# Gate weights in two K halves, an earlier gate transfer, and one parameter transpose at the start of an SSM + SwiGLU kernel

## Chip, cores, metric

The kernel runs on one core of one Trainium2 chip. The metric is device time in microseconds (us). Each kernel is run several times. One execution of each is also profiled; the profile's "span" is some 1.8 us shorter than the time. All runs used here are fast, and that only means that a run isn't over 1.5% above the fastest of its kernel.

## The reference, cut to what matters

```python
xn = layernorm(x)                                   # x: 2048 x 512, bf16
A  = 2 * Re(C @ scan(Lam_bar, B_bar @ xn)) + xn * Dskip   # state space part, P = 512
B  = (silu(xn @ w_gate) * (xn @ w_up)) @ w_down           # F = 1376
out = x + A + B
```

The sequence is worked in four chunks of 512 rows. Only the start of chunk 0 is changed: four tiles of x (128 x 512 each) are loaded, normalized and transposed on chip, and the first six tiles of `w_gate` (6 x 128 of the 1376 columns) are multiplied with them, tile by tile of x ("quarters"). K is the dimension that is summed over, here the 512 columns of x in four K tiles of 128. "Gate" and "up" loads and matmuls are those of `w_gate` and `w_up`; the matmuls write to PSUM. Later chunks of x are transposed by DMA.

## The kernel before

The loads, in issue order on two queues (SyncE is the default, `eng="act"` is ScalarE's queue):

```python
FQ = 4 * 128                                       # FH0 = 6 * 128
act_q = [pload("ld_ldt", 2, A_log_dt)]             # 1 KB, ScalarE's queue
dma("ld_x0", ...); dma("ld_x1", ...)               # 128 KB each, SyncE
act_load("ld_wgA0", wg[:, 0:2, 0:FQ], ...)         # 256 KB, K tiles 0-1, ScalarE
dma("ld_x2", ...)
act_load("ld_wgA1", wg[:, 2:4, 0:FQ], ...)         # 256 KB, K tiles 2-3, ScalarE
dma("ld_wg0", wg[:, :, FQ:FH0], ...)               # 256 KB, SyncE
dma("ld_x3", ...)
pload("ld_lim", ...); pload("ld_lre", ...)         # 1 KB each, ScalarE
dma("ld_wu0", ...); dma("ld_wg1", ...); dma("ld_wu1", ...); dma("ld_x4", ...)
# ... later: transposing loads of B (2), of xn chunk 1, of C (2), then x tiles 8-11
```

TensorE's start: warm-up matmuls on a constant, the transposes of tile 0 in two halves, three more warm-ups, then the quarters:

```python
pe_warm(10)
xt_tile_fine(0, parts=2, wbank=...)      # half, 1 warm-up, half; each half copied by ScalarE
pe_warm(3, 256, ...)
for q in range(4):
    for ii, (i, bk) in enumerate(tiles):                    # six tiles
        if q == 0 and ii == 2:
            params_t(...)                                   # three 4x128 transposes
            ln_chunk0_rest(...)
        if q < 3 and ii == (4 if q == 0 else 2):
            xt_tile_fine(q + 1)                             # next tile: 4 transposes, one copy
        # ... 4 matmuls over K for tile i, quarter q
```

A small scheduler orders the instructions of VectorE, ScalarE and GpSimd by estimates; TensorE and SyncE keep the order of the program.

## Time and profile before

| | before |
|---|---|
| time, median of 3 runs | 180.34 us (180.32 to 180.59) |
| span of the profiled run | 178.4 us |
| TensorE busy / on the chain that ended last | 98% / 95% |
| first gate weight load / first up matmul on the chain | 6.03 / 13.15 us |

The prediction shows the chain of waits and the weight-load row. One more view is needed below, the timeline of VectorE (start, length, engine, line, operation, output and inputs, count, and in brackets the idle time ahead and what ended it):

```profile
2.95 0.69 DVE L466 BATCH_NORM_STATS2 st<-x_sb 128x6 f32<-128x512 bf16 x1 [2.95 <-DMA x_sb<-in_A_x_dram]
...
3.96 0.68 DVE L466 BATCH_NORM_STATS2 st<-x_sb 128x6 f32<-128x512 bf16 x1
4.74 0.60 DVE L485 TENSOR_SCALAR xn_sb<-x_sb,mv,rstd 128x256 bf16<-128x256 bf16 x2
```

The first line is tile 0's arrival, 2.95. The second is tile 1. The third is both halves of tile 0's normalization.

### The profile page before, as it was taken

The numbers are of one execution on the slowest core, as the hardware profiler recorded it, in microseconds if no ns is written. First come the engines' busy times: TensorE is split into PE (matmuls) and PEld (weight loads), VectorE is DVE, ScalarE is ACT, GpSimd is POOL, SyncE is SP. The second block draws the span as 40 slices with busy tenths as digits, with TensorE's granted clock in tenths as the row PEclk, the third lists the DMA queues.
The fourth block names the chain that finished last, engine by engine and source line by source line (L and its number), as shares of the span: only waits on it lengthen the run. The fifth ranks groups of instructions, "written<-read, shape, count | busy, mean of one in ns | idle before, by whom it ended". The sixth has DMA issues, their size and how long they took to land.

```text
span 178.4 us, 2380 instructions
## 1 busy us (share of the span) xinstructions
PE 174.3 (98%) x919; PEld 83.6 (47%) x927; DVE 160.8 (90%) x273; ACT 86.5 (48%) x107; POOL 12.7 (7%) x24
## 2 busy tenths in 40 slices
PE   8899999999999999999999999999999999999994
PEld 2694444444444444444444444444444444444743
DVE  3987759998799999999999999999999999999733
ACT  3379899899796991061565651000965620000000
POOL 3351300002200000300000000000000000000000
PEclk9999999999999999999999999999999999999999
DMA  4994646669360000002420000001100000001112
GB/s 152 343 365 103 142 82 73 152 174 353 108 118 4 0 0 0 0 0 91 101 48 0 0 0 4 0 0 65 53 0 4 0 0 0 0 0 62 44 44 88
DMA packets 23410, 12.37 MB, mean 69 GB/s; under 512 B 15112, under 2 KB 23400, under 8 KB 23400
## 3 DMA queue, kind: packets, MB, share of 16 engines
q1 hardware_dynamic: 22832, 11.70, 24.5%
q10 hardware_dynamic: 568, 0.53, 1.0%
q8 instruction: 7, 0.11, 0.3%
q14 instruction: 3, 0.02, 0.0%
HBM read 6.46 MB, written 2.10 MB: 48 GB/s over the span
## 4 chain that ended last, share of the span: by engine, by line
PE 95%; DMA 1%; DVE 1%; issue 1%; ACT 0%; POOL 0%
PE pb L713 36%; PE pb L901 21%; PE pb L818 15%; PE pb L914 15%; PE pb L752 3%; PE pb L781 2%; DMA x_sb<-in_A_x_dram 1%; PE pb L791 1%; PE pb L543 1%; DVE st L466 0%; ACT xnT L549 0%; POOL rstd L478 0%; PE pb L450 0%; DVE xn_sb L485 0%; DVE x_sb L919 0%
## 5 line engine op out<-in xcount | busy, mean ns | idle before, releaser
L858 DVE TENSOR_TENSOR_SCAN rot<-sm,car,rot 128x512 bf16<-128x512 f32 x32 | 39.0, 1266 | 0.1
L901 PE MATMUL pb<-wd,hT 128*128 128x512 bf16 (+3 forms) x194 | 38.1, 355 | 0.2
L713 PE MATMUL pb<-xnT,wu 128*128 128x512 bf16 x160 | 37.3, 379 | 0.0
L713 PE MATMUL pb<-xnT,wg 128*128 128x512 bf16 x136 | 32.0, 379 | 0.0
L914 PE MATMUL pb<-W,hss 128*128 128x512 bf16 (+2 forms) x140 | 28.1, 355 | 0.2
L818 PE MATMUL pb<-xnT,BT 128*128 128x512 bf16 x128 | 28.1, 379 | 0.0
L901 PEld LDWEIGHTS pb<-wd,hT 128*128 128x128 bf16 (+1 forms) x198 | 18.5, 98 | 19.9
L725 ACT ACTIVATE sg<-pb 128x1024 bf16<-128x1024 f32 x20 | 20.2, 1022 | 10.9 <-PE pb L713 10.6
L713 PEld LDWEIGHTS pb<-xnT,wu 128*128 128x128 bf16 x160 | 15.6, 98 | 18.6
L771 ACT ACTIVATE uf<-pb 128x1024 bf16<-128x1024 f32 x20 | 20.4, 1022 | 7.1 <-PE pb L713 6.6
L713 PEld LDWEIGHTS pb<-xnT,wg 128*128 128x128 bf16 x136 | 13.2, 98 | 16.4 <-issue 0.8
L914 PEld LDWEIGHTS pb<-W,hss 128*128 128x128 bf16 x144 | 13.5, 98 | 14.3
L818 PEld LDWEIGHTS pb<-xnT,BT 128*128 128x128 bf16 x128 | 12.5, 98 | 15.1
L825 ACT ACTIVATE u_sb<-pb 128x1024 bf16<-128x1024 f32 x16 | 16.3, 1026 | 3.9 <-PE pb L818 3.5
L919 DVE TENSOR_TENSOR x_sb<-pb,x_sb 128x512 bf16<-128x512 f32 (+2 forms) x18 | 10.9, 621 | 4.9 <-PE pb L914 4.9
L773 DVE TENSOR_TENSOR hT<-sg,uf 128x1024 bf16<-128x1024 bf16 x20 | 13.4, 676 | 1.9 <-ACT uf L771 1.9
L466 DVE BATCH_NORM_STATS2 st<-x_sb 128x6 f32<-128x512 bf16 x16 | 10.2, 683 | 4.9 <-DMA x_sb<-in_A_x_dram 4.9
L495 ACT ACTIVATE xn_sb<-x_sb,nmr,rstd 128x512 bf16<-128x512 bf16 x8 | 5.9, 802 | 10.0 <-DVE nmr L492 10.0
L800 ACT ACTIVATE sg<-pb 96x1024 bf16<-96x1024 f32 x2 | 2.0, 1020 | 17.4 <-PE pb L781 17.4
L849 DVE TENSOR_TENSOR rot<-u_sb,sin 128x2048 bf16<-128x2048 bf16 x8 | 9.7, 1214 | 0.0
L849 DVE TENSOR_TENSOR rot<-rot,sin 128x2048 bf16<-128x2048 bf16 x8 | 9.7, 1214 | 0.0
L849 DVE TENSOR_TENSOR rot<-u_sb,cosT 128x2048 bf16<-128x2048 bf16 x8 | 9.7, 1212 | 0.0
(71 smaller groups left out, 138.6 us busy)
## 6 DMA issues: line engine op xcount, KB each, us to landing
out_dram<-x_sb SPq DMA_DIRECT2D x15, 128.0 KB, 1.7
x_sb<-in_A_x_dram SPq DMA_DIRECT2D x3, 512.0 KB, 7.4
wd<-in_B_w_down_dram SPq DMA_DIRECT2D x1, 1280.0 KB, 7.0
wu<-in_B_w_up_dram SPq DMA_DIRECT2D x1, 768.0 KB, 6.4
wg<-in_B_w_gate_dram SPq DMA_DIRECT2D x1, 608.0 KB, 7.7
wu<-in_B_w_up_dram SPq DMA_DIRECT2D x1, 608.0 KB, 8.8
x_sb<-in_A_x_dram SPq DMA_DIRECT2D x4, 128.0 KB, 3.0
wg<-in_B_w_gate_dram ACTq DMA_DIRECT2D x2, 256.0 KB, 3.8
```

What stands on the lines that cost most here:

```text
L466: return g.add("dve", lambda e, a=a: e.bn_stats(out=st[:, a, :], in_=x_sb[:, a, :]), reads=[("x", a)], writes=[("st", a)], name="bnst%d" % ...
L713: inst = e.matmul(pbank[0:fs, bk, :].rearrange("p (j t) -> p j t", j=4), lhsT=w[:, kt, i * 128:i * 128 + fs], rhs=xnT[:, c % 2, :, kt, :], ...
L725: g.add("act", lambda e: e.activation(out=sg[rows, sl, 0:n, :].rearrange("p a t -> p (a t)"), in_=pair_f32(rows, bk, 512 * n), func=AF.Sil ...
L771: g.add("act", lambda e: e.activation(out=uf[rows, ul, 0:n, :].rearrange("p a t -> p (a t)"), in_=pair_f32(rows, bk, 512 * n), func=AF.Ide ...
L773: g.add("dve", lambda e: e.tensor_tensor(out=hT[rows, hb, i0:i0 + n, :], in0=sg[rows, sl, 0:n, :], in1=uf[rows, ul, 0:n, :], op=ALU.mult), ...
L818: inst = e.matmul(pbank[:, bk, :].rearrange("p (j t) -> p j t", j=4), lhsT=BT[:, ri, kt, pt * 128:(pt + 1) * 128], rhs=xnT[:, c % 2, :, kt ...
L825: g.add("act", lambda e: e.activation(out=u_sb[:, us].rearrange("p r t -> p (r t)"), in_=pair_f32(slice(0, 128), b0), func=AF.Identity), r ...
L849: tt = lambda out, a, b, op, r, w, nm: g.add("dve", lambda e: e.tensor_tensor(out=out, in0=a, in1=b, op=op), reads=r, writes=w, name="%s_% ...
L858: g.add("dve", lambda e, A0=A0, A1=A1, k=k, ri=ri, pt=pt: e.tensor_tensor_scan(out=A1[:, k, ri, :], data0=rr[:, pt:pt + 1].to_broadcast([1 ...
L901: inst = e.matmul(pbank[:, bk, 0:nc_], lhsT=hT[0:fs, hb, i, lt * 128:(lt + 1) * 128], rhs=wd[0:fs, i, c0:c0 + nc_], start=(i == 0), stop=F ...
L914: inst = e.matmul(pbank[:, bk, 0:nc_], lhsT=hss[:, hb, pt, ri, lt * 128:(lt + 1) * 128], rhs=W12[:, ri, pt, c0:c0 + nc_], start=False, sto ...
L919: g.add("dve", lambda e, bk=bk, a=a, c0=c0, nc_=nc_: e.tensor_tensor(out=x_sb[:, a, c0:c0 + nc_], in0=pbank[:, bk, 0:nc_], in1=x_sb[:, a, ...
```

## The change

The intent: start the gate matmuls with the first half of K as soon as half of tile 0 and half of the weights are there, close the hole at the edge of each quarter, and take the parameter transposes out of the gate stream.

```diff
-        FQ = 4 * 128
-        act_q = [pload("ld_ldt", 2, A_log_dt)]
         dma("ld_x0", ...); dma("ld_x1", ...)
-        act_load("ld_wgA0", wg[:, 0:2, 0:FQ], ...)
+        act_q = [dma("ld_wgA0", wg[:, 0:2, 0:FH0], ..., 256 * FH0 * 2, eng="act")]
+        act_q.append(dma("ld_wgA1", wg[:, 2:4, 0:FH0], ..., eng="act", order=(act_q[-1],)))
+        pload("ld_ldt", 2, A_log_dt)              # SyncE
+        pload("ld_lim", 1, A_Lambda_im)
+        pload("ld_lre", 0, A_Lambda_re)
         dma("ld_x2", ...)
-        act_load("ld_wgA1", ...); dma("ld_wg0", ...)
         dma("ld_x3", ...)
-        act_q.append(pload("ld_lim", ...)); act_q.append(pload("ld_lre", ...))
 ...
-        pe_warm(10)
+            pe_warm(9, bk=wbank)
+            ln_first()                            # stats 0, stats 1, first half of tile 0
+            xt_tile_fine(0, bridge=bridge)        # half; params_t and rest of layernorm; half
+            pe_warm(1, 256, wbank)
             for q in range(4):
+                steps = [(i, bk, 2 * kh, 2 * kh + 2) for kh in range(2) for i, bk in tiles]
+                #  (last quarter: halves for two tiles, whole K for four)
+                for n, (i, bk, k0, k1) in enumerate(steps):
+                    if q < 3 and n == 8:
+                        xt_tile_fine(q + 1)       # two copies of half a tile
```

The three parameter rows now lie in one 12 x 128 tile and are transposed by one instruction. (Some order hints for ScalarE and VectorE are cut here.)

## The prediction

> **What bounds the kernel now.** I read the page first, for the engine that carries the end. The busy shares and the chain that ended last:
>
> ```profile
> PE 174.3 (98%) x919; PEld 83.6 (47%) x927; DVE 160.8 (90%) x273; ACT 86.5 (48%) x107; POOL 12.7 (7%) x24
> ...
> PE 95%; DMA 1%; DVE 1%; issue 1%; ACT 0%; POOL 0%
> ```
>
> TensorE is the bound: 95% of the chain. DMA, VectorE and the rest together hold 5% of 178.4 us, about 9 us, at the two ends. The change touches only the first 13 us, so next I read the chain in order of time there (start, length, what):
>
> ```profile
> 0.79 2.13 DMA x_sb<-in_A_x_dram
> ...
> 6.06 0.69 PE pb L752 x8
> 6.76 0.08 issue
> 6.83 0.21 PE pb L457 x3
> 7.04 0.55 PE pb L752 x8
> 7.60 0.24 PE pb L543 x4
> 7.86 0.61 ACT xnT L549
> 8.46 0.05 issue
> 8.51 0.62 PE pb L752 x8
> ...
> 10.92 2.23 PE pb L752 x40
> 13.15 12.09 PE pb L713 x56
> ```
>
> Until 6.06 the chain is x tile 0, its layernorm, its transpose and its copy out of PSUM. From 6.06 to 13.15 are the 96 small gate matmuls, and they are interrupted twice. From 13.15 TensorE has no hole: 56 up matmuls take 12.09 us, 216 ns each. The weight-load row of the timeline shows the interruptions best[...]:
>
> ```profile
> 6.03 0.55 PEld L752 LDWEIGHTS pb<-xnT,wg 128*128 128x128 bf16 x8 [0.27 <-DMA wg<-in_B_w_gate_dram]
> 6.80 0.15 PEld L457 LDWEIGHTS pb<-ident,prow 4*128 4x128 bf16 x3 [0.22 <-issue]
> 6.97 0.45 PEld L752 LDWEIGHTS pb<-xnT,wg 128*128 128x128 bf16 x8
> ...
> 8.51 0.45 PEld L752 LDWEIGHTS pb<-xnT,wg 128*128 128x128 bf16 x8 [0.41 <-ACT xnT L549]
> ```
>
> The first gate load waited 0.27 us for weights, three parameter transposes stand in the stream, and the second quarter waited 0.41 us for the ScalarE copy of tile 1. The duration of that copy, by form (256 wide is the shortest, 512 the median):
>
> ```profile
> L549 ACT ACTIVATE xnT<-pb x5: 377/597/597, 5.5 to 11.0; 128x512 bf16<-128x512 bf16 x3, 128x256 bf16<-128x256 bf16 x2
> ```
>
> **What the Trainium skill says.** "DMA: Bandwidth & Descriptors", section "Issuing engines are not separate DMA queues": transfers started by SyncE and ScalarE run on the same 16 DMA engines and interleave; another issuer saves only issue time. The trace agrees: in the half-microsecond table DMA is 95% busy or more from 3.5 to 6.5 us while both issuers are active. The same page, "Queues, rings and completion order", has each engine alternate between queues packet by packet; no view of this trace shows packets of one transfer. "TensorE: Matmul & The Clock Gate", Part 1, gives 107 ns per 128-column matmul cold and 56 ns warm, with some 3.4 us of activity to warm. Here ten 512-wide warm-up matmuls come 0.43 us apart, the cold rate, and the 40 gate matmuls in 2.23 us are 56 ns each, the warm one; the clock turned at about 5.2 us. The clock row says full speed throughout, so it doesn't show this and only durations do.
>
> **The change, part by part.**
>
> First, the parameter transposes. Removed from the gate stream: three, with the hole ahead of them. On the weight-load row that is the hole 0.22 plus 0.15 plus 0.02 until the next gate load, 0.39 us on TensorE's path. Added: one 12x128 transpose between the two halves of tile 0, where TensorE waits for VectorE anyway. It needs three tiny transfers that SyncE now issues as numbers 3 to 5. Issues there are about 0.45 us apart from 0.79, so the last leaves at about 2.6; with the 2.1 us that x tile 0 took it lands at about 4.7, before the first transpose at 5.23. Cost expected on the path: 0.
>
> Second, halves of K. The six tiles of a quarter first take K 0-1, then K 2-3: 12 matmuls of 56 ns, 0.67 us, need only the first half of the copy and of the weights. A whole-tile copy of 0.60 us becomes two of 0.38, so the first matmul can start 0.22 us sooner after it. The next tile's transposes also move ahead of 8 matmuls at the end of each quarter, 8 x 56 = 0.45 us, against a first copy of 0.38 plus a few hundredths of hand-over. So the 0.41 us hole should close. The second copy (another 0.38) lies beside the 0.67 us of first halves. The split first tile also lost about 0.08 us (8 matmuls in 0.69 us where later groups take 0.62); that goes. Matmuls and transposes stay as many: 96 x 56 ns + 12 x 55 ns = 6.04 us, against 7.09 now.
>
> Third, the order of VectorE. The second half of tile 0 moves behind the statistics of tile 1: 0.17 + 0.15 us with 0.04 between, so about 0.35 later. Its transpose goes to about 5.75 and its copy ends near 6.35; the matmuls that need it come at 6.03 + 0.67 = 6.70. Hidden. Tile 1 then needs parameter copy 0.17, statistics of tile 2 0.68 and normalization 0.41 after about 5.65: ready near 6.95. Its transposes are wanted 16 x 56 = 0.89 us after the first gate matmul, 6.92-6.95. This is almost equal, so I charge 0.1 us for a remaining hole. Later tiles cost VectorE 0.68+0.41+0.17+0.15, 1.41 us, below TensorE's 24 x 56 + 4 x 55, 1.56 us: no further hole.
>
> Fourth, transfers. The first gate half grows from 256 to 384 KB and leaves ScalarE at 0.79 instead of 1.38, because the little parameter load (0.56 us) no longer stands before it. The weights' 0.27 us wait should end. But x tile 0 leaves at the same 0.79, and a fine view of DMA rates shows that it moved at 300 to 420 GB/s around 2.2-2.5 us, nearly alone. With a gate transfer beside it, it gets about half: 128 KB at some 400 GB/s is 0.3 us, so it comes up to 0.3 us later, 0.25 charged. It heads the chain, so all behind it moves. The first gate matmul is then bound by the copy of tile 0: that ended at 5.54 + 0.38 = 5.92 and now near 6.17; with hand-over the first load is at about 6.2 instead of 6.03, a loss of 0.17 us.
>
> **The sum.** Gains 0.39 + 0.41 + 0.08 = 0.88; losses 0.17 + 0.10 = 0.27; net about 0.6 us. The gate stage should run from about 6.2 to 12.5 instead of 6.06 to 13.15. Behind it TensorE has no hole to fill or make: the up weights (issued at 3.20, landing 6.4 us later, 9.6) are early; the transposed B matrices land at 19.02 + 4.9 = 23.9, and their second half is needed at 25.24 + 0.86 = 26.1; the last scan output ends at 164.9 against its use at 169.1. Each slack is larger than 0.6, so the gain should reach the end: 180.34 - 0.6 = 179.7 us.
>
> **Rivals.** (a) *The wait turns into a DMA wait.* Before its second gate half the chip must move 768 KB of gate weights and 256 to 512 KB of x, some 1.0 to 1.3 MB; summing the half-microsecond rates of before, 1.05 MB had moved by 5.5 us and 1.34 MB by 6.5. The need is at about 6.85. Usually enough, by little; x tile 2, issued near 2.9 instead of 1.7, is also close to its use at 5.9. If this goes wrong, 0.3 to 0.6 us return: 180.0 to 180.3. (b) *Start later than charged*, because x tile 0 loses more, or the parameter transfer is late and blocks TensorE's in-order stream before the second half: 180.2 or a little over. (c) *Clock*: nine warm-ups end at about 4.7, leaving 0.5 us idle instead of 0.24. If the turn is put off, matmuls cost 107 instead of 56 ns for some time: +0.05 us each, 1.7 us over a 3.4 us window, thus about 181.4. Against it: 3.8 us of warm-up is still over the skill's 3.4. (d) *The gain is hidden later*: VectorE is almost 100% busy from 50 to 150 us. Against it are the slacks above. It would give 180.3. (e) *No charge is real*, full gain: 179.4.
>
> **Range and chances.** (a), (b), (d) fill 180.0 to 180.4, (e) and a weight wait that I undervalued 179.2 to 179.5. Three runs of before differ by 0.27 us. Range 179.1 to 180.5. A 2% change is 3.6 us; the whole of 6.06-13.15 holds only 1.05 us of holes, and the whole clock risk is 1.7. Faster by over 2%: 0.01; within 2%: 0.98; slower: 0.01.
>
> **What the profile after would show.** The first gate weight load at 6.1 to 6.3, released by the copy and not by DMA; no load of parameters inside the gate stream; no ScalarE release of over 0.1 us in it; the first up matmul at 12.4 to 12.7; statistics of tile 0 starting at 3.1 to 3.25 instead of 2.95; an unbroken TensorE chain from then on. Wrong would be: a gate load released by the weights' or x's DMA for over 0.2 us, gate matmuls 107 ns apart, or a hole after 13 us that was not there.

## The result, and the profile after

The changed kernel took 181.57 us (median of 6, 180.83 to 181.88), the kernel before in the same rounds 180.5 (6 runs, 180.32 to 180.97). Ratio 1.0051, 95% interval 1.0026 to 1.0076. A ratio is the mean time of one kernel's fast runs over that of the other's in the same rounds, so it is not quite the ratio of the medians. By the 2% rule that is "same", but it is slower, about 1.9 us over the forecast of 179.7 and outside its range. The profiled run of the changed kernel was the slowest of its six (181.88), so the 1.7 us explained below are that run's; the medians differ by 1.07.

The chain of waits of the changed kernel, in order of time (start, length, what):

```profile
1.25 3.59 DMA x_sb<-in_A_x_dram
...
5.96 0.37 PE pb L538 x2
6.33 0.12 PE pb L449
6.45 0.35 PE pb L538 x2
6.79 0.21 PE pb L444
7.01 1.71 PE pb L756 x16
8.71 0.43 PE pb L538 x4
9.14 1.92 PE pb L756 x24
...
14.87 12.09 PE pb L709 x56
```

The first up matmul stands at 14.87 instead of 13.15: 1.72 us later, and the span is 1.7 us longer (180.1 for 178.4). So the whole loss is made in the first 15 us. The first line is the transfer of x tile 1. L538 are transposes of x, L449 the parameter transpose, L756 the gate matmuls. The first 16 gate matmuls take 1.71 us, 107 ns each; the 40 gate matmuls at the end of the gate stage before took 56 ns each. Four transposes take 0.43 instead of 0.22.

TensorE's matmul and weight-load rows in its timeline, two answers:

```profile
5.96 0.37 PE L538 MATMUL pb<-ident,xn_sb 128*128 128x128 bf16 x2 [1.13 <-DVE mv L461]
```

```profile
6.80 1.65 PEld L756 LDWEIGHTS pb<-xnT,wg 128*128 128x128 bf16 x16 [0.17 <-ACT xnT L544]
...
14.65 1.23 PEld L709 LDWEIGHTS pb<-xnT,wu 128*128 128x128 bf16 x7
```

The first up load of the kernel before, for comparison:

```profile
12.93 0.37 PEld L713 LDWEIGHTS pb<-xnT,wu 128*128 128x128 bf16 x3
```

TensorE stood still for 1.13 us ahead of its first transpose. The first gate load is at 6.80 (before: 6.03), and the first up load at 14.65 (before: 12.93), so the gate stage takes 7.85 us instead of 6.90. The 1.72 us are thus 0.77 of later start and 0.95 of a longer stage. VectorE's timeline says why the start is late:

```profile
3.43 0.69 DVE L457 BATCH_NORM_STATS2 st<-x_sb 128x6 f32<-128x512 bf16 x1 [3.43 <-DMA x_sb<-in_A_x_dram]
...
4.87 0.69 DVE L457 BATCH_NORM_STATS2 st<-x_sb 128x6 f32<-128x512 bf16 x1 [0.34 <-DMA x_sb<-in_A_x_dram]
5.48 0.33 DVE L488 TENSOR_SCALAR xn_sb<-x_sb,mv,rstd 128x256 bf16<-128x256 bf16 x1
```

Tile 0 arrives 0.48 us later than before. Tile 1 also arrives late (4.85), and as its statistics stand ahead of tile 0's normalization in VectorE's order, that normalization begins at 5.48 instead of 4.74.

What the clock does isn't visible in the clock row of this profile, which reads full speed throughout; only the 107 ns tell.

### The profile page after: what moved, and what is told of

Its sections match the earlier page's. It is cut to its first block, busy times and chain, and to the rows that moved or that the text cites. A ratio compares the mean times of both kernels' runs of the same rounds, so it can differ in the third digit from the quotient of the medians.

```text
span 180.1 us, 2383 instructions
## 1 busy us (share of the span) xinstructions
PE 175.8 (98%) x921; PEld 84.8 (47%) x921; DVE 160.5 (89%) x273; ACT 87.1 (48%) x110; POOL 12.7 (7%) x24
## 4 chain that ended last, share of the span: by engine, by line
PE 95%; DMA 2%; DVE 1%; SPq 0%; issue 0%
PE pb L709 36%; PE pb L906 21%; PE pb L919 15%; PE pb L823 15%; PE pb L756 4%; DMA x_sb<-in_A_x_dram 2%; PE pb L786 2%; PE pb L796 1%; PE pb L538 1%; DVE st L457 0%; SPq L384 0%; DVE x_sb L924 0%; DVE xn_sb L488 0%; PE pb L444 0%; PE pb L449 0%
## 5 line engine op out<-in xcount | busy, mean ns | idle before, releaser
L863 DVE TENSOR_TENSOR_SCAN rot<-sm,car,rot 128x512 bf16<-128x512 f32 x32 | 38.9, 1265 | 0.0
L906 PE MATMUL pb<-wd,hT 128*128 128x512 bf16 (+3 forms) x198 | 38.8, 355 | 0.0
```

The lines of the kernel that those rows point to most:

```text
L863: g.add("dve", lambda e, A0=A0, A1=A1, k=k, ri=ri, pt=pt: e.tensor_tensor_scan(out=A1[:, k, ri, :], data0=rr[:, pt:pt + 1].to_broadcast([1 ...
L906: inst = e.matmul(pbank[:, bk, 0:nc_], lhsT=hT[0:fs, hb, i, lt * 128:(lt + 1) * 128], rhs=wd[0:fs, i, c0:c0 + nc_], start=(i == 0), stop=F ...
```

## Experiments

Theory 1 (clock): the hole ahead of the first transpose keeps TensorE's clock slow into the gate stage. Theory 2 (data): late x tiles and weights alone explain the loss. Times are medians (lowest to highest), ratios to the kernel before of the same chip and rounds.

| run | time, us | ratio (95%) |
|---|---|---|
| e1: 13 warm-ups | 180.88 (180.52 to 181.38) | 1.0024 (1.0005 to 1.0043) |
| e2: gate transfer later again | 181.04 (180.61 to 183.07) | 1.0022 (1.0004 to 1.0041) |
| e3: before with 7 warm-ups | 181.41 (180.35 to 182.6) | 1.0046 (1.0013 to 1.008) |
| e4: tile 0 ahead of tile 1 | 181.95 (180.57 to 182.54) | 1.0068 (1.0037 to 1.01) |
| e5: repaired version | 180.46 (180.13 to 180.91) | 1.0002 (0.9981 to 1.0023) |
| e6: e5, gate transfer at once | 180.48 (180.38 to 180.91) | 1.0005 (0.9987 to 1.0024) |
| e7: e5, whole K | 181.68 (181.26 to 182.36) | 1.0071 (1.0049 to 1.0093) |
| e8: changed kernel again | 181.79 (180.74 to 182.2) | 1.0062 (1.0036 to 1.0088) |
| e9: e5, x tiles 8-11 earlier | 180.42 (180.21 to 181.5) | 1.0006 (0.9986 to 1.0026) |
| e10: before, x tiles 8-11 earlier | 180.72 (180.4 to 180.92) | 1.0014 (1.0 to 1.0028) |
| e11: e9, gate weights shared out | 180.01 (179.87 to 180.31) | 0.9974 (0.996 to 0.9988) |
| e12: e11, x tiles 8-11 late again | 180.71 (180.45 to 182.29) | 1.0034 (1.0 to 1.0067) |
| e13: e11 again | 180.21 (179.75 to 180.62) | 0.9978 (0.9957 to 0.9999) |

All results were correct. e1 to e4 shared a chip and rounds (before: 180.45, 180.03 to 181.06), as did e5 to e8 (before: 180.46), e9 and e10 (180.41), and e12 and e13 (180.52); e11 ran by itself (180.51).

### e1: fill the hole

```diff
-            pe_warm(9, bk=wbank)
+            pe_warm(13, bk=wbank)
```

> The changed kernel with 13 instead of 9 warm-up matmuls, so that TensorE has no hole of 1.13 us ahead of its first transpose (4.83 to 5.96 us in the changed kernel's trace). Theory 1 (clock): the hole put off the turn from 107 to 56 ns per gate matmul until about 10.2 us. Then here nearly all gate matmuls come 56 ns apart, the gate stage takes 6.2 to 6.4 us from its first load, the first up matmul stands at 13.0 to 13.4 and the time is 179.9 to 180.5, spread some 0.6. Theory 2 (data): the slow gate matmuls and the later end come from late x tiles and late weights, filling the hole changes nothing: first up matmul at about 14.9, time 181.2 to 181.8.

The x tiles were nearly as late as in the changed kernel (statistics at 3.25 and 4.82, there 3.43 and 4.87), and TensorE's weight-load row reads:

```profile
6.65 0.90 PEld L756 LDWEIGHTS pb<-xnT,wg 128*128 128x128 bf16 x16
...
12.97 2.96 PEld L709 LDWEIGHTS pb<-xnT,wu 128*128 128x128 bf16 x15
```

The stage takes 12.97 - 6.65 = 6.32 us with the same data order and nearly the same late x, against 7.85. The 16 loads take 0.90 instead of 1.65. So 1.53 us of the changed kernel's stage are the slow clock, and without it the stage is 0.58 shorter than before (6.90). A count without e1 agrees: by the chain of the changed kernel some 27 gate matmuls took 107 instead of 56 ns, and four transposes 0.43 instead of 0.22 us, together 1.6 us. Theory 2 fell in the profile. But the two profiles are the fastest of e1's six runs and the slowest of the changed kernel's. The times fell by less: the ratio from 1.0051 to 1.0024, some 0.5 us (0.7 by the medians, which are of different rounds), and the two intervals overlap. The 180.88 is above the expected 180.5; part of that is explained by e5.

### e3: make the hole in the kernel before

```diff
-    warm=10,
+    warm=7,
```

> The kernel before with 7 instead of 10 warm-up matmuls and nothing else: a hole of about 1.4 us ahead of the first transpose at 5.23, as the changed kernel has, with the old data order and the old transfers. Clock theory: gate matmuls 107 ns apart until some time between 8.5 and 12, +1 to +2 us: 181.3 to 182.4. Data theory: same time as before, 180.2 to 180.8.

The time went from 180.45 to 181.41. The stretches of the profiled run (length, TensorE busy and instructions, granted clock, DMA share, GB/s) show the clock here, because it changes twice within the run. The first fence is its first transpose:

```profile
5.17 0.27 PE L543 MATMUL pb<-ident,xn_sb 128*128 128x128 bf16 x2 [1.39 <-DVE xn_sb L485]
```

```profile
6.00:6.50 0.50, 0.50 (x8) 1.00 1.30 308
6.50:7.00 0.50, 0.20 (x4) 0.87 0.78 264
7.00:7.50 0.50, 0.44 (x7) 0.50 1.03 349
...
10.00:11.00 1.00, 1.00 (x18) 0.86 1.08 359
```

The gate matmuls began at the full clock, dropped to half at about 6.9 and came back at about 10.3, some 3.4 us later. TensorE had stood still for 1.39 us before its first transpose (and the drop falls into a second hole, of 0.36 us from 6.70 on). Only three warm-ups had been left out, so in this run a hole of this size was enough. Not every run pays: the six runs were 180.35, 180.53 and 181.4 to 182.6.

### e8: the changed kernel again

> The changed kernel once more, on the chip and in the rounds of its repaired versions. Clock theory: its time depends on where the turn of the clock falls, which differs from run to run, so a spread of 1 us or more (180.5 to 182.5), median 181.3 to 181.8, and a first up matmul in the profile anywhere from 13.2 to 15. Data theory: spread as small as that of the kernel before (0.3 to 0.6 us) and the gate matmuls slow in every profile.

Six runs between 180.74 and 182.2; with the first six, twelve between 180.74 and 182.2, a spread of 1.46 us. The spread is what the clock theory had said. The profile again has the first 16 gate matmuls in 1.71 us and the first up matmul at 14.79; slow gate matmuls in both profiles are what both theories allow. By the distances of the matmul starts, the turn to 56 ns falls at 10.2 and 10.0 in the two profiles of this kernel, at 4.9 in e1, at 3.8 in e5: it isn't tied to the kernel's start. "TensorE: Matmul & The Clock Gate", Part 1, of the Trainium skill offers a reason: the activity window is 3.4 us long and free-running. The runs agree with it: in all profiles but those of the changed kernel and e2 the first turn fell between about 3.5 (e12) and 6.7 us (e10), less than one window apart. That the window is the cause no run here shows.

### e2: give x its head start back

```diff
-        act_q = [dma("ld_wgA0", ...)]
+        act_q = [pload("ld_ldt", 2, A_log_dt, eng="act")]
+        act_q.append(dma("ld_wgA0", ..., order=(act_q[-1],)))
-        pload("ld_ldt", 2, A_log_dt)
```

> The changed kernel with one small parameter load put back on ScalarE's queue ahead of the gate weights, so that the gate weights leave about 0.55 us after x tile 0 as before (and SyncE issues one transfer less ahead of x tile 2). If the gate transfer beside it made x tile 0 late, its statistics start at 2.95 to 3.1 again instead of 3.43 and those of tile 1 don't wait for its transfer; first transpose at 5.2 to 5.4, hole ahead of it 0.4 to 0.6 us. By the clock theory the clock then turns in time or nearly so: first up matmul 12.4 to 13, time 179.6 to 180.2. By the data theory alone the first up matmul moves by the 0.7 us of the x tiles only: 14.2, time 180.9. If x tile 0 stays at 3.4, the delay has another cause than the neighbour. The order of later VectorE work changes a little with this edit; TensorE's chain after 13 us should stay without holes.

The statistics of tile 0 began at 2.85 and those of tile 1 at 3.86 without a wait: the gate transfer beside them is what made x late. But the first up matmul came at 16.06 in the profiled run, which was the slowest of the seven (the other six took 180.61 to 181.1). Its chain has a new wait, and its weight loads show the slow clock, until about 12.6:

```profile
5.12 0.37 PE pb L538 x2
5.50 1.06 issue
6.55 0.16 PE pb L449
```

```profile
9.08 2.61 PEld L756 LDWEIGHTS pb<-xnT,wg 128*128 128x128 bf16 x24
```

The gate stage took 9.0 us (from 6.84 to 15.84), so the clock did not turn in time as expected: the hole had only moved behind the first transposes. L449 is the parameter transpose. It stands ahead of the second half's transposes in TensorE's program, and TensorE stood still 1.06 us in front of it although the second half of tile 0 was normalized by 5.52. The profile names no releaser here; in e4's it names the parameter transfers (0.57 us for one of them). The last of these 1 KB loads was issued at 2.13 us in e2 and 2.41 in e4, and TensorE began with them only at 6.52 and 6.26.

### e4: tile 0's normalization ahead of tile 1's statistics

```diff
-            last = bn_st(1, order=(last,))
-            hold["last"] = ln_half(0, 0, order=(last,))
+            last = ln_half(0, 0, order=(last,))
+            hold["last"] = bn_st(1, order=(last,))
```

> The changed kernel with the first half of tile 0's normalization ahead of the statistics of tile 1 on VectorE, so that the late transfer of x tile 1 (landing 4.85) no longer holds the first transpose. First transpose at about 5.5 instead of 5.96, hole 0.7 instead of 1.13 us. Data theory: 0.45 us sooner, if tile 1 doesn't become the limit: 181.1; as tile 1's chain is unchanged, the gain can shrink to 0. Clock theory: the same, unless a hole of 0.7 us no longer puts off the clock's turn; then 179.7 to 180.3.

The first transpose moved to 5.60 as expected, but the first gate load stayed at 6.89: the second half of tile 0 waits behind tile 1's statistics, and the parameters held TensorE until 6.26. The profiled run had the fast clock throughout, other runs took up to 182.54, the three slowest with a mean granted clock of 0.991. So this is no repair; the hole was only cut into pieces.

### e5 and e6: repaired, and what the head start costs

The repaired version has e2's edit, the other two small loads behind x tile 3, the parameter transpose after the second quarter, and two short warm-ups in its old place:

```diff
             def bridge():
-                params_t(pbk)
-                ln_chunk0(pbk)
+                pe_warm(2, 256, wbank)
+                ln_chunk0()                     # without the parameter copy
-            pe_warm(9, bk=wbank)
+            pe_warm(10, bk=wbank)
 ...
+                if q == 1:
+                    params_t(xt_pair[0]); ln_rest(xt_pair[0])
```

> The changed kernel with three repairs: one small parameter load ahead of the gate weights on ScalarE's queue (x tiles 0 and 1 get their head start), the other two small loads behind x tile 3 and the parameter transpose after the second quarter (in the run with the head start alone it blocked TensorE until 6.5 us), ten warm-ups and two short ones between the halves of tile 0. Theory: late x tiles plus holes that put off the clock's turn ate the gain; with both gone the first gate load comes at about 6.0, the gate stage takes 6.2 us, first up matmul at 12.2 to 12.6, time 179.4 to 180.0, ratio to the kernel before 0.994 to 0.997. Rival (weights): with the gate weights 0.5 us later the second half of K now waits for its weights; first up matmul 12.8 or later, ratio 0.998 to 1.000.

> As the repaired version, but the gate weights again leave at once (the small load goes to SyncE behind x tile 3), with 13 warm-ups to fill the longer wait for tile 0. This isolates what the head start of the gate weights costs when no hole is left to blame: if the gate transfer beside x is the cause, statistics of tile 0 at 3.25 to 3.45 and of tile 1 waiting until about 4.8, first gate load 6.6 to 6.8, about 0.7 us later than in the repaired version, time 180.1 to 180.7. If x tiles come late for another reason, the two versions are equal.

In e5 the front worked as expected: first gate load at 5.90, first up load at 12.54 (before 12.93). In e6, with the gate transfer at once, the statistics are back at 3.61 and 5.00, the first gate load at 6.76 and the first up load at 13.21. So the head start is worth 0.67 to 0.86 us to the front, and it was the neighbour that delayed x. But both took the same time, 180.46 and 180.48. e5 lost its lead later, in two rows of its timeline (the first fence ScalarE, the second weight loads):

```profile
46.80 2.93 ACT L481 ACTIVATE xn_sb<-x_sb,nmr,rstd 128x512 bf16<-128x512 bf16 x4 [1.96 <-DVE nmr L478]
49.63 1.00 ACT L781 ACTIVATE uf<-pb 128x1024 bf16<-128x1024 f32 x1
```

```profile
50.68 1.41 PEld L711 LDWEIGHTS pb<-xnT,wu 128*128 128x128 bf16 x8 [1.07 <-ACT uf L781]
```

Four normalizations of x tiles 8 to 11 stand in one block on ScalarE, and the copy that frees PSUM comes after them. TensorE's weight loads wait 1.07 us, where the kernel before has no hole. The cost is less: from the first up matmul (12.75 on the chain) to the end e5 takes 178.8 - 12.75 = 166.05 us, the kernel before 178.4 - 13.15 = 165.25, so 0.8 us were lost. Those x tiles land at 41.2 us, because their load comes after five transposing loads that run one after the other from 14.85 us on; this chain doesn't get shorter when TensorE starts sooner (before, they landed at 40.6). The weight loads of e1 and e4 have the same hole (0.63 and 0.81 us); e6, whose tiles happened to land by 38.9, has none.

### e7: the repaired version with whole K

```diff
-                    steps = [(i, bk, 2 * kh, 2 * kh + 2) for kh in range(2) for i, bk in tiles]
+                steps = [(i, bk, 0, 4) for i, bk in tiles]
-                    if q < 3 and n == 8:
+                    if q < 3 and n == 4:
```

> The repaired version with the gate matmuls of a tile over the whole K again, six groups of four in each quarter (the copies out of PSUM stay in halves). If the halves of K close the hole at the quarter's edge, this version has holes of 0.2 to 0.4 us at the second quarter and starts its first gate matmuls about 0.3 us later: first up matmul 0.5 to 0.9 us later, time +0.4 to +0.9 over the repaired version. If the halves of K give nothing, the two are equal within 0.2 us.

The weight-load row has the holes that the halves close:

```profile
6.81 0.91 PEld L755 LDWEIGHTS pb<-xnT,wg 128*128 128x128 bf16 x16 [1.04 <-ACT xnT L546]
...
8.75 0.90 PEld L755 LDWEIGHTS pb<-xnT,wg 128*128 128x128 bf16 x16 [0.36 <-ACT xnT L546]
```

The first up load comes at 13.93 against 12.54, and the time is 181.68 against 180.46. The halves of K are worth 1.2 us in this arrangement (1.39 at the first up load, of which e5 loses more later), more than the 0.4 to 0.9 expected, probably because the start needs all 768 KB of weights. (The 1.04 us are put down to the copy, which had ended at 6.31. The weights' second half is the likelier releaser: in e5, with the same loads, the matmuls that need it began at 6.74. The profile doesn't name it.)

### e9 and e10: move the later load

```diff
         def loads_stage_b2():
+            dma("ld_x8", x_sb[:, 8:12, :], ...)
             dma("ld_cre", ..., xpose=True)
             dma("ld_cim", ..., xpose=True)
-            dma("ld_x8", x_sb[:, 8:12, :], ...)
```

> The repaired version with the load of x tiles 8 to 11 moved ahead of the two transposing loads of C, instead of behind them. Theory (second wall): in the repaired version those tiles land at 41.2 us, so that their four normalizations sit on ScalarE at 46.8 to 49.7 and hold the copies out of PSUM; TensorE then waited 1.07 us at 50.7 and lost what it had gained in the first 13 us. Here the tiles land at about 31.5 to 32, the normalizations run earlier, the wait at 50.7 is gone and the span is the first up matmul (12.5 to 12.8) plus 165.2: 177.7 to 178.2, time 179.4 to 180.0, ratio to the kernel before 0.994 to 0.998. Rival: the wait only moves (ScalarE is short of time for tables and copies anyway, or the B and C matrices come late), and the time stays at 180.3 to 180.6.

> Control: the kernel before with the same move of the load of x tiles 8 to 11 and nothing else. It has no hole on TensorE at 50 us, so the move alone should give nothing: time within 0.2 us of the kernel before, ratio 0.999 to 1.001, first up matmul at 13 as before. If it gains as much as the repaired version does, the load order is a change of its own and says nothing on where the gain of the first 13 us went.

e9 has no hole at 50 us any more; its normalizations now lie between 37 and 42.7. But it took 180.42, as its front had a hole of its own:

```profile
7.45 0.24 PEld L758 LDWEIGHTS pb<-xnT,wg 128*128 128x128 bf16 x4 [0.65 <-issue]
```

Its chain puts this down to the gate weights, which landed at 7.34. In e5 the same hole was 0.16. The control e10 gained nothing (ratio 1.0014, a little over the expected 1.001), so the moved load alone is no gain. Its profile also shows that the start of the kernel before varies: its clock turned only at about 6.7, and its first up matmul stood at 13.70, not at 13.15. The time of e9 by itself couldn't show that the hole at 50 mattered, as its front was late too.

### e11, e12, e13: both at once, and the later wall alone

e11 shares the second half of the gate weights out:

```diff
-        act_q.append(dma("ld_wgA1", wg[:, 2:4, 0:FH0], ..., eng="act"))
+        act_q.append(dma("ld_wgA1", wg[:, 2:3, 0:FH0], ..., eng="act"))
 ...
+        dma("ld_wgA2", wg[:, 3:4, 0:FH0], ...)     # SyncE, behind x3, ahead of the up weights
```

> The version of the run before last (repairs, x tiles 8 to 11 loaded earlier), with the second half of the gate weights shared out: K tile 2 stays on ScalarE's queue, K tile 3 goes on SyncE's queue behind x tile 3 and ahead of the up weights. In the run without this TensorE waited 0.65 us at 7.45 for the second half, which landed only at 7.34 us because the up weights moved at the same time. If that contention is the cause, the hole at the second half of K is under 0.1 us here, first up matmul 12.3 to 12.8 us, no hole at 50 us, span 177.6 to 178.1, time 179.3 to 180.0, ratio to the kernel before 0.994 to 0.998. If x and gate weights together are simply too many bytes for the time (1.28 MB), the hole stays at 0.3 us or more and the time at 180.2 to 180.5.

e12 is e11 with x tiles 8 to 11 loaded late again (e9's diff undone); e13 is e11 once more beside it.

> The best version so far with the load of x tiles 8 to 11 back behind the transposing loads of C. Its front is the same, so if the later wall is real, this one starts the up matmuls as early but has a hole of 0.3 to 1.1 us on TensorE near 50.7 us (the four ScalarE normalizations at 46 to 50 ahead of a copy), and is 0.3 to 0.8 us slower than the best version on the same chip, thus back at 180.3 to 180.7. If the wall was only an accident of one schedule, the two are equal within 0.2 us.

> The best version once more, for the same chip and rounds as its partner: 179.8 to 180.3, ratio to the kernel before 0.996 to 0.999, no hole on TensorE after its first up matmul, whose time plus 165.2 gives the span.

e11 took 180.01, ratio 0.9974: the first version whose interval lies below the kernel before, by some 0.5 us ("same" by the 2% rule). Its profiled run was the slowest of five, with tile 1 late by 0.58 us and the first up load at 13.08. e12 and e13 on one chip took 180.71 and 180.21. Their weight-load rows, e12 first:

```profile
50.60 1.41 PEld L712 LDWEIGHTS pb<-xnT,wu 128*128 128x128 bf16 x8 [0.73 <-ACT uf L782]
```

```profile
12.51 4.90 PEld L712 LDWEIGHTS pb<-xnT,wu 128*128 128x128 bf16 x24
...
49.70 1.61 PEld L712 LDWEIGHTS pb<-xnT,wu 128*128 128x128 bf16 x8
```

e12 starts the up loads at 12.80, and they wait 0.73 us at 50.6; by its chain (first up matmul at 13.02, span 178.7) this cost 0.4. e13 starts them at 12.51 and has no hole at 49.7; its span is 178.0, of which the first up matmul (12.73 on the chain) makes all the difference to before: 178.0 - 12.73 = 165.3, and 178.4 - 13.15 = 165.3. So in these profiles a gain of the front reaches the end whole only with the later load moved too. The 0.5 us between the two medians is not the wall alone: of the 0.7 us between the two spans, 0.3 is the later front of e12. The weights are not quite settled: e12, with the same shared-out loads, still waited 0.48 us for them, and e13 not at all.

## Why the prediction was wrong

**What bounds the kernel** was right: TensorE's chain is whole after 15 us in the changed kernel, and its span moved by what its first up matmul moved by.

**The parameter transposes** did leave the gate stream. But the step that made them free ("lands at about 4.7") was wrong: it took the 2.1 us of a first, lonely transfer for a 1 KB transfer behind others under load. e2 and e4 show 6.5 and 6.3. In the changed kernel TensorE waited only 0.20 us there, and the second half of tile 0 was no earlier, as x was late as well.

**The halves of K** were right in kind: the hole of 0.41 us behind ScalarE's copy is gone, e7 brings such holes back, and the stage without clock loss takes 6.32 us (e1), so 0.58 less than before, where the sum had 0.88 - 0.10 = 0.78, which includes the parameter transposes.

**The transfers** were undersized. 0.25 us were charged for tile 0 and it was 0.48. Tile 1 wasn't charged at all: before, it arrived ahead of its use; now it arrived at 4.85, and **the order of VectorE** put that wait ahead of tile 0's normalization. The first gate load came at 6.80, not at 6.2. e2 and e6 against e5 show that the earlier gate transfer is the cause.

**The clock** is the step that turned a small loss into the result. Rival (c) was named with its mechanism and its cost (about 1.7 us), but with a hole of 0.5 us and against it the count of warm-ups. That count did not protect: in the changed kernel all nine ran at the slow rate, and the clock had not turned when they ended at 4.83. (The turn in the kernel before was read as 5.2; its tenth warm-up starts 0.41 us after the ninth and the transposes at 5.23 come 0.05 apart, which puts it near 4.6.) The late x tiles made that hole 1.13 us, and the cost was 1.53. The two risks had been treated as separate; one caused the other. Sum: +0.77 start, -0.58 stage, +1.53 clock = 1.72, the measured shift of the up matmuls. It closes by construction, as the last two terms both come from e1's stage; the count of slow matmuls (1.6 us) is the independent check.

**"Each slack is larger than 0.6"** was wrong as well, though the changed kernel never came to it. The list of slacks left out x tiles 8 to 11 and the block of normalizations on ScalarE. e5 ran into that wall with a lead of 0.4 us and lost 0.8 us there; the profile of e12 loses 0.4 and that of e13 nothing. Rival (d) looked for the wall on VectorE.

**Still open:** where the clock's turn falls was read off single profiles. The timed runs tell a part: each has a mean granted clock, and eight read 0.991, three of the changed kernel's twelve, three of e4's six and two of e3's six. They took 181.4 to 182.54 us. No other run of any kernel reads below 0.999, and these three kernels are the ones with a hole of 0.77 us or more ahead of the first transpose. Over 180 us, 0.009 is some 3.2 us at half clock, about the slow stretch of e3. But other slow runs read full clock, among them the profiled 181.88 and e2's 183.07, whose matmuls were slow all the same, and two runs of e12 (181.56 and 182.29) that nothing explains. So how much of each timed run's spread is the clock and how much the arrival of tile 1 and of the weights isn't separated.

## What to carry to other kernels

When a transfer is moved up, ask first whose share of the DMA it takes: the item that heads the dependency chain should leave alone, and the bulk behind it half a microsecond later (0.55 us here). At a cold start count every hole on TensorE as a risk to its clock, and keep instructions that wait on a small, late transfer out of its in-order stream. Before counting a gain at the start, look for the next place where the bound engine's margin is zero for a reason that doesn't move with it, here a chain of loads that ends in a block of work on ScalarE.

## What the Trainium skill lacked or had wrong

- "TensorE: Matmul & The Clock Gate", Part 1: its table has the clock return to half "after ≥1 idle window (~3.4µs)". Here the clock returned to half, from about 6.9 to 10.3 us, after a hole of only 1.39 us (e3). In the changed kernel, whose clock had not turned yet, a hole of 1.13 us was followed by 107 ns per matmul until about 10.2. The length of e3's slow stretch agrees with the page's window. Its remark that the ramp costs under 1% also holds (1.53 of 181 us), but that was more than the whole change was worth.
- The same page, Part 4, gives about 275 ns for a transpose in a kernel and says that the full clock doesn't engage for it. Here a transpose's record is 0.22 us long at the fast clock and mostly 0.31 at the slow one, and four came in 0.22 and in 0.43 us: they followed the clock.
- "DMA: Bandwidth & Descriptors", Anatomy of one DMA, gives a fixed cost of some 2 us, for transfers that GpSimd issues; those here are issued by SyncE and ScalarE. No page has a figure for a 1 KB transfer queued behind large ones: loads issued by 2.13 us (e2) and 2.41 us (e4) were used at 6.52 and 6.26, over 3.8 us later.
- The same page, "Issuing engines are not separate DMA queues", says that a second issuer saves only issue time, and that the transfers interleave. It has no number for what this takes from the transfer that heads the chain: a 384 KB transfer issued on ScalarE at the same moment brought x tile 0 in at 3.25 to 3.61 us instead of 2.85 to 2.99 (start of the statistics, five profiles against ten).
- The first page, Part 1, warns that the clock events of a trace are not fully to be trusted. It doesn't say that the clock row can read full speed while the matmuls come at the slow pace, as in the changed kernel; among the profiles kept, only e3's shows the half clock.
